# Decode attention block on one core: slots laid on multiples of 512 bytes, and the bias columns taken out of the first load

## The chip, the cores and the metric

The kernel runs on one core of one Trainium2 chip. The metric is the device time of one launch in microseconds (us). Before the change it is 1057.04 us, the median of 3 runs (1056.93 to 1057.11). About a difference of 0.2% can be told from no change.

## The reference

One token goes through a transformer block whose scales and shifts come from a condition vector `c`. All data are float32. Cut to what matters:

```python
mod = (silu(c) @ w_mod).reshape(1, 6, 1, 640)      # sa, ca, ga, sb, cb, gb
h = layernorm(x) * (1 + ca) + sa
q = (h @ wq), 32 heads of 192
p = softmax(q . k_cache * 192**-0.5)               # k_cache: 32 heads x 8192 keys x 192
x = x + ga * ((p . v_cache) @ wo)                  # v_cache: the same size
h = layernorm(x) * (1 + cb) + sb
x = x + gb * (relu(h @ w1 + b1)**2 @ w2 + b2)      # 640 -> 1536 -> 640
```

The two caches are 403 MB of the 452 MB that are read. Each byte of them is used once.

## The kernel before, in words

**Slots.** All large operands pass through three buffers, the slots (pool `strm`, 56,832 bytes in each of 128 partitions). They are filled in turn, by one DMA each or by a few: `first_t` (weights of the first modulation, the first pair's query weights, and small columns), then `k0`, `v0`, `k1`, `v1` and so on through 32 heads, then the weights of the second half. A slot is loaded again when what lay in it has been used. The pools are laid out in the order in which they are opened: `const` first, so the slots begin at byte 36,640 of a partition, which is 71 x 512 + 288.

**Issue order.** SP (SyncE) issues every DMA, in the order of the code: lines 63 (`first_t`), 95 (keys) and 99 (values). An issue that must wait holds up all that stand behind it on SP. It waits for two sorts of things. One is the engines that still read the slot. The other is the DMA's own completion semaphore: the framework gives the DMAs of SP eight semaphores in turn (`DMAHW0` to `DMAHW7` in the order of instructions below). The ninth DMA takes the first one's semaphore again, and is issued only when that first DMA has landed.

**Start.** When `first_t` has landed, ScalarE, VectorE and TensorE make the modulation, the layernorm and the first query `qb` (lines 163 to 197). VectorE then copies out `x` and the biases `bbc` over 32 lanes and transposes them (`spread`, lines 107 to 113, called on 198 and 199); they are first needed in the second half. Then comes the first head.

**A head.** VectorE multiplies the keys by the query in place (line 214), GpSimd folds part of the products (215), VectorE and ScalarE sum them (218 to 222); softmax (225 to 241); TensorE multiplies by the values (243 to 260); `own` and `turn` gather the head's output. The key slot is free after the sums on line 222, and the value slot after TensorE's last product on line 258.

**The biases** `B_b1` and `B_b2` (17 columns) are the last columns of `first`, and line 169 copies them into `bbc`.

Of the kernel before, what the change touches and what calls it, by code (L numbers as in the profile page):

```python
# [8 lines left out]
F32 = mybir.dt.float32  # L9
# [4 lines left out]
P = 128  # L14
D = 640
# [7 lines left out]
KB = DG // 32  # L23
FB = FG // 32
# [5 lines left out]
WQ = KB * PW  # L30
ROW = KV + WO
WM = KB * 2 * D
VEC = 3 * KB + FB
DA = 128
DB = DH - DA
REP = 8
# [6 lines left out]


@with_exitstack
def block_kernel(ctx: ExitStack, tc: tile.TileContext, first, kx, vx, wm1, w1, w2, out):
    nc = tc.nc
    const = ctx.enter_context(tc.tile_pool(name="const", bufs=1))
    strm = ctx.enter_context(tc.tile_pool(name="strm", bufs=3))
    work = ctx.enter_context(tc.tile_pool(name="work", bufs=2))  # L50
    psum = ctx.enter_context(tc.tile_pool(name="psum", bufs=1, space=bass.MemoryType.PSUM))
    ctx.enter_context(tc.manual_schedule())
# [1 line left out]
    def slot(name):  # L54
        return strm.tile([P, ROW], F32, tag="slot", name=name, bufs=3)

    def big(name, n):
# [4 lines left out]
    first_t = slot("first_t")  # L62
    nc.sync.dma_start(first_t[:, :WM + WQ + VEC], first)

# [1 line left out]
    make_identity(nc, ident)  # L66
    ones = const.tile([P, P], F32, name="ones")
    nc.vector.memset(ones, 1.0)
    eps_t = const.tile([P, 1], F32, name="eps_t")
    nc.vector.memset(eps_t, EPS)  # L70

    mask = const.tile([P, 2 * 512], F32, name="mask")
# [3 lines left out]
                            axis=AX.X, op=ALU.add)  # L76
# [3 lines left out]
                            axis=AX.X, op=ALU.add)  # L80
# [3 lines left out]

    vec = first_t[:, WM + WQ:WM + WQ + VEC]
    c_c = vec[:, :KB]
    x_c = const.tile([P, KB], F32, name="x_c")
    bbc = const.tile([P, FB + KB], F32, name="bbc")

    def load_k(h):  # L90
        k_t[h] = slot(f"k{h}")
        n = K_PARTS.get(h, 1)
        cuts = [KV * c // n for c in range(n)] + [ROW if h in WO_AT or h in WQ_AT else KV]
        for a, b in zip(cuts, cuts[1:]):
            nc.sync.dma_start(k_t[h][:, a:b], kx[h, :, a:b])
# [63 lines left out]
            nc.vector.scalar_tensor_tensor(to, w[:, j], s[:, j:j + 1], to, op0=ALU.mult, op1=ALU.add)  # L159

    load_k(0)

    e = const.tile([P, KB], F32, name="silu")
    nc.scalar.activation(e, c_c, AF.Exp, scale=-1.0)
# [1 line left out]
    nc.vector.reciprocal(e, e)  # L166
    nc.vector.tensor_mul(e, e, c_c)
    nc.vector.tensor_copy(x_c, vec[:, KB:2 * KB])
    nc.vector.tensor_copy(bbc, vec[:, 2 * KB:])

    ca1 = const.tile([P, KB], F32, name="ca1")
    sa = const.tile([P, KB], F32, name="sa")
# [268 lines left out]
```

## Time and profile before

| | |
|---|---|
| median of 3 runs | 1057.04 us |
| profiled execution, its own time | 1056.98 us |
| its span, first to last instruction | 1055.2 us |
| read from HBM | 451.82 MB, 428 GB/s over the span |
| DMA queue's share of 16 engines | 99.3% |
| VectorE busy | 904.1 us (86%) |
| TensorE busy, mean granted clock | 368.2 us (35%), 0.652 |

The profile is of one execution. Its own time is 1.8 us longer than its span, and 0.06 us under the median. "Share of 16 engines" adds up the times of the packets over the core's sixteen DMA engines. Where a row ends in `<-X`, the engine stood idle until X had ended. SPq is SP's queue of DMA issues, and a row of it is the issue alone, not the transfer.

### The profile page before, as it was taken

What the parts mean: (1) busy time and instruction counts of PE and PEld (TensorE: products, weight loads), DVE (VectorE), ACT (ScalarE), POOL (GpSimd) and SP (SyncE); (2) the same over time, 40 slices, a digit from 0 to 9 for tenths busy, and PEclk for the clock granted to TensorE, in tenths of its full rate; (3) what the DMA queues carried; (4) which work ended last, traced back from release to release, by engine and by line L of the source; (5) the groups of instructions that cost most, each with busy time, mean ns of one, the idle gap of its engine ahead of it and who ended that gap; (6) DMA issues with size and microseconds to landing.
All of it is one profiled execution on the core that took longest, in us unless ns stands there. A gap on an engine that the chain in (4) does not pass through costs nothing.

```text
span 1055.2 us, 5497 instructions
## 1 busy us (share of the span) xinstructions
PE 368.2 (35%) x2120; PEld 133.4 (13%) x2120; DVE 904.1 (86%) x398; ACT 89.4 (8%) x360; POOL 199.4 (19%) x44
## 2 busy tenths in 40 slices
PE   1224333243431334343143432224343133433346
PEld 0101101011110111111011110101111011110113
DVE  7887898998989989898998988989898998989982
ACT  1010000000000000000000000000000000012230
POOL 0220222220122221122221022221022222022110
PEclk9666656666665666656666665666666566666568
DMA  9999999999999999999999999999999999999997
GB/s 403 437 438 422 438 433 429 441 420 443 419 443 430 428 437 437 418 445 431 424 443 431 426 431 436 432 437 426 437 425 440 430 436 428 432 429 431 432 426 314
DMA packets 10834, 452.16 MB, mean 429 GB/s; under 512 B 1205, under 2 KB 1209, under 8 KB 1593
## 3 DMA queue, kind: packets, MB, share of 16 engines
q1 hardware_dynamic: 10808, 451.83, 99.3%
q8 instruction: 16, 0.26, 0.1%
q14 instruction: 10, 0.07, 0.0%
HBM read 451.82 MB, written 0.00 MB: 428 GB/s over the span
## 4 chain that ended last, share of the span: by engine, by line
DMA 39%; DVE 35%; PE 14%; POOL 9%; issue 1%; ACT 1%; POOLq 0%; SPq 0%; DVEq 0%; ACTq 0%
DMA k<-in_kx 36%; DVE k L214 21%; POOL k L215 9%; PE ps_o L254 9%; DVE sc L222 5%; DVE os L281 3%; PE ps_o L258 3%; DMA w_t<-in_w 2%; DVE own L277 2%; DVE sc L219 1%; DMA first_t<-in_first 1%; PE ps_mx L229 1%; PE ps_oT L287 1%; DVE ma_w L152 1%; PE ps_q L193 1%
## 5 line engine op out<-in xcount | busy, mean ns | idle before, releaser
L214 DVE TENSOR_TENSOR k<-k,qb 128x12288 f32<-128x12288 f32 (+2 forms) x37 | 415.4, 11227 | 88.6 <-DMA k<-in_kx 84.4
L215 POOL TENSOR_TENSOR k<-k 128x2880 f32<-128x2880 f32 (+2 forms) x37 | 198.1, 5354 | 813.7 <-DVE k L214 762.8
L229 PE MATMUL ps_mx<-ident,mp 128*128 128x128 f32 x32 | 15.2, 474 | 587.2 <-DVE mp L227 587.2
L219 DVE TENSOR_REDUCE sc<-k 128x32 f32<-128x6144 f32 (+5 forms) x37 | 201.5, 5445 | 1.3
L254 PE MATMUL ps_o<-v,p 128*32 128x512 f32 x1024 | 186.4, 893 | 2.6 <-ACT p L237 2.6
L222 DVE TENSOR_REDUCE sc<-k 128x30 f32<-128x2880 f32 (+2 forms) x37 | 99.7, 2696 | 5.2 <-POOL k L215 4.7
L218 ACT ACTIVATE jk<-k 128x192 f32<-128x192 f32 x127 | 44.5, 351 | 519.7 <-DVE k L214 508.5
L229 PEld LDWEIGHTS ps_mx<-ident,mp 128*128 128x128 f32 x32 | 5.8, 182 | 611.9 <-DVE mp L227 590.9
L281 DVE TENSOR_REDUCE os<-own 128x128 f32<-128x512 f32 x64 | 63.9, 1038 | 1.1
L258 PE MATMUL ps_o<-v,p 128*32 128x512 f32 x496 | 58.6, 592 | 0.0
L254 PEld LDWEIGHTS ps_o<-v,p 128*32 128x32 f32 x1024 | 40.6, 155 | 118.3 <-issue 114.9
L193 PE MATMUL ps_q<-k,ln_h 128*128 128x384 f32 x150 | 52.3, 496 | 0.2 <-DMA k<-in_kx 0.2
L237 ACT ACTIVATE p<-sc,nm 128x512 f32<-128x512 f32 x32 | 23.1, 721 | 321.6 <-DVE nm L231 180.5
L159 DVE SCALAR_TENSOR_TENSOR acc<-k,oT,acc 128x640 f32<-128x640 f32 x45 | 41.5, 923 | 1.1
L287 PE MATMUL ps_oT<-ones,os 128*128 128x1 f32 x96 | 27.2, 356 | 42.5 <-DVE os L281 30.3
L193 PEld LDWEIGHTS ps_q<-k,ln_h 128*128 128x128 f32 x150 | 27.3, 189 | 28.2 <-issue 10.9
L287 PEld LDWEIGHTS ps_oT<-ones,os 128*128 128x128 f32 x96 | 23.3, 304 | 50.3 <-DVE os L281 32.9
L231 DVE TENSOR_REDUCE nm<-ps_mx 128x1 f32<-128x128 f32 x32 | 9.3, 292 | 18.3 <-PE ps_mx L229 18.3
L218 ACT ACTIVATION_READ_ACCUMULATOR jk<-k 128x1 f32 x127 | 23.7, 187 | 0.0
L258 PEld LDWEIGHTS ps_o<-v,p 128*32 128x32 f32 x496 | 14.9, 110 | 40.0 <-issue 40.0
L277 DVE SCALAR_TENSOR_TENSOR own<-ps_o,mask 128x1024 f32<-128x1024 f32 x16 | 19.4, 1215 | 0.0
L277 DVE SCALAR_TENSOR_TENSOR own<-ps_o,ri,mask 128x1024 f32<-128x1024 f32 x15 | 19.2, 1277 | 0.0
(91 smaller groups left out, 126.5 us busy)
## 6 DMA issues: line engine op xcount, KB each, us to landing
k<-in_kx SPq DMA_DIRECT2D x28, 7104.0 KB, 27.3
v<-in_vx SPq DMA_DIRECT2D x32, 6144.0 KB, 22.7
k<-in_kx SPq DMA_DIRECT2D x2, 6144.0 KB
k<-in_kx SPq DMA_DIRECT2D x2, 4032.0 KB, 26.5
k<-in_kx SPq DMA_DIRECT2D x2, 3072.0 KB, 17.3
first_t<-in_first SPq DMA_DIRECT2D x1, 4173.5 KB, 12.7
wm_t<-in_wm SPq DMA_DIRECT2D x1, 3840.0 KB
w_t<-in_w SPq DMA_DIRECT2D x1, 3840.0 KB, 19.2
```

Of the source, the lines that this page charges most:

```text
L159: nc.vector.scalar_tensor_tensor(to, w[:, j], s[:, j:j + 1], to, op0=ALU.mult, op1=ALU.add)
L193: nc.tensor.matmul(ps[:, :PW], h1[:, b:b + 1].to_broadcast([P, P]), w[:, b], start=(b == 0), stop=(b == KB - 1))
L214: nc.vector.tensor_mul(pr, pr, q[:, None, :].to_broadcast([P, n, DH]))
L215: nc.gpsimd.tensor_add(pr[:, a:b, :DH // 2], pr[:, a:b, :DH // 2], pr[:, a:b, DH // 2:])
L218: nc.scalar.activation(jk, pr[:, i], AF.Copy, accum_out=s[:, i:i + 1])
L219: nc.vector.tensor_reduce(s[:, :a], pr[:, :a], axis=AX.X, op=ALU.add)
L222: nc.vector.tensor_reduce(s[:, a:b], pr[:, a:b, :DH // 2], axis=AX.X, op=ALU.add)
L254: nc.tensor.matmul(oa[32 * g:32 * (g + 1)], p[:, 4 * c:4 * c + 4].rearrange("p e r -> p (e r)"), t[:, 512 * c:512 * (c + 1)], start=(c < G ...
L258: nc.tensor.matmul(ob[32 * g:32 * (g + 1)], p[:, 8 * c:8 * c + 8, ::2].rearrange("p e r -> p (e r)"), t[:, 512 * (na + c):512 * (na + c + ...
L277: nc.vector.scalar_tensor_tensor(m, o, scale, mask, op0=ALU.mult, op1=ALU.mult)
L281: nc.vector.tensor_reduce(r, m[:, lo:hi].rearrange("p (j d) -> p d j", d=r.shape[1]), axis=AX.X, op=ALU.add)
L287: nc.tensor.matmul(pt[:, j:j + 1], os_[:, P * j:P * (j + 1)], ones[:, :1], start=True, stop=True)
```

## The change

1. **Layout.** A new pool `base` is opened first and holds only `eps_t`, on 384 bytes; then come the slots, and `const` after them. The slots now begin at byte 16,896 of a partition, 33 x 512; their size, 111 x 512 bytes, is as before. The tiles in `const` and `work` get other addresses.
2. **Bias columns.** They leave `first` (8,330 columns in place of 8,347) and become an input `bb` of their own. It is read by sixteen DMAs of 8, 1, 2, 3, ... 15 rows of 68 bytes, issued on SP behind `k0` and ahead of `v0`, straight into `bbc`. VectorE's copy on line 169 goes.

```diff
-VEC = 3 * KB + FB
+VEC = 2 * KB
...
+    base = ctx.enter_context(tc.tile_pool(name="base", bufs=1))
+    eps_t = base.tile([P, 96], F32, name="eps_t")[:, :1]
+    strm = ctx.enter_context(tc.tile_pool(name="strm", bufs=3))
     const = ctx.enter_context(tc.tile_pool(name="const", bufs=1))
-    strm = ctx.enter_context(tc.tile_pool(name="strm", bufs=3))
     work = ctx.enter_context(tc.tile_pool(name="work", bufs=2))
...
-    eps_t = const.tile([P, 1], F32, name="eps_t")
     nc.vector.memset(eps_t, EPS)
...
     load_k(0)
+    r0 = 0
+    for n in [8] + list(range(1, 16)):
+        nc.sync.dma_start(bbc[r0:r0 + n], bb[r0:r0 + n])
+        r0 += n
...
     nc.vector.tensor_copy(x_c, vec[:, KB:2 * KB])
-    nc.vector.tensor_copy(bbc, vec[:, 2 * KB:])
...
-        "first": np.concatenate([rows(wm[:, :2 * D], KB), wq[0], column(c, KB), column(A_x, KB),
-                                 column(B_b1, FB), column(B_b2, KB)], axis=1),
+        "first": np.concatenate([rows(wm[:, :2 * D], KB), wq[0], column(c, KB), column(A_x, KB)], axis=1),
...
+        "bb": np.concatenate([column(B_b1, FB), column(B_b2, KB)], axis=1),
```

SP's issues at the start of the program before, with the semaphores that each waits for in brackets (`DMAHW0` to `DMAHW7` are those of the DMAs; the others are the engines'):

```order
L63 DMA first_t_69<-in_first 128x8347
L95 DMA k0_88<-in_kx 128x14208
L99 DMA v0_152<-in_vx 128x12288
L95 DMA k1_205<-in_kx 128x12288 [waits DVE_49,DMAHW0_49,PE_49,Activation_49]
L99 DMA v1_207<-in_vx 128x12288 [waits DVE_49,DMAHW1_49,PE_49,Activation_49]
```

The first three have nothing to wait for. The same queue now, from the seventh small load (the ninth DMA) to `k1`; ahead of these stand `first_t`, `k0` and the small loads of 8 and of 1 to 5 rows, which wait for nothing:

```order
L165 DMA bbc_90<-in_bb 6x17 [waits DMAHW0_49]
L165 DMA bbc_90<-in_bb 7x17 [waits DMAHW1_49]
L165 DMA bbc_90<-in_bb 8x17 [waits DMAHW2_49]
L165 DMA bbc_90<-in_bb 9x17 [waits DMAHW3_49]
L165 DMA bbc_90<-in_bb 10x17 [waits DMAHW4_49]
L165 DMA bbc_90<-in_bb 11x17 [waits DMAHW5_49]
L165 DMA bbc_90<-in_bb 12x17 [waits DMAHW6_49]
L165 DMA bbc_90<-in_bb 13x17 [waits DMAHW7_49]
L165 DMA bbc_90<-in_bb 14x17 [waits DMAHW0_49]
L165 DMA bbc_90<-in_bb 15x17 [waits DMAHW1_49]
L100 DMA v0_170<-in_vx 128x12288 [waits DMAHW2_49]
L96 DMA k1_223<-in_kx 128x12288 [waits DVE_49,DMAHW3_49,PE_49,Activation_49]
```

`DMAHW0` is `first_t`'s semaphore and `DMAHW1` is `k0`'s, so the load of 6 rows waits for `first_t` and the load of 7 rows waits for `k0`; `v0`, which was third, is now nineteenth. On VectorE, the place between the spread of `x` and the first product of keys, before:

```order
L110 COPY x_t_c<-x_c 128x160
L112 STREAM_TRANSPOSE x_t<-x_t_c 128x160 [waits DVE_49]
L110 COPY bbt_c<-bbc 128x544 [waits DVE_49]
L112 STREAM_TRANSPOSE bbt<-bbt_c 128x544 [waits DVE_49]
L214 TENSOR_TENSOR k_88<-k_88,qb_142 128x12288 [waits DMAHW1_49,Activation_49]
```

and now:

```order
L111 COPY x_t_c<-x_c 128x160
L113 STREAM_TRANSPOSE x_t<-x_t_c 128x160 [waits DVE_49]
L111 COPY bbt_c<-bbc 128x544 [waits DMAHW4_49,DMAHW3_49,DMAHW5_49,DMAHW2_49,DMAHW6_49,DMAHW1_49,DMAHW7_49,DMAHW0_49,DVE_49]
L113 STREAM_TRANSPOSE bbt<-bbt_c 128x544 [waits DVE_49]
L218 TENSOR_TENSOR k_91<-k_91,qb_160 128x12288 [waits Activation_49]
```

The order is the same, but the copy of the biases, ahead of the first product, now waits for all sixteen small loads.

## Rows read from the trace of the kernel before

**Rows 1.** The page: busy time of each engine, and the DMA queue's bytes and share.
```profile
PE 368.2 (35%) x2120; PEld 133.4 (13%) x2120; DVE 904.1 (86%) x398; ACT 89.4 (8%) x360; POOL 199.4 (19%) x44
...
q1 hardware_dynamic: 10808, 451.83, 99.3%
```

**Rows 2.** Chain that ended last, in order of time: start us, us, what.
```profile
0.74 12.69 DMA first_t<-in_first
...
154.31 12.97 DVE k L214
...
217.10 12.97 DVE k L214
...
1026.98 24.16 DMA w_t<-in_w
```

**Rows 3.** DMA issues from 0 to 45 us: KB each, us to landing.
```profile
k<-in_kx SPq DMA_DIRECT2D x1, 7104.0 KB, 29.0
v<-in_vx SPq DMA_DIRECT2D x1, 6144.0 KB, 43.1
...
first_t<-in_first SPq DMA_DIRECT2D x1, 4173.5 KB, 12.7
```

**Rows 4.** SP's queue from 0 to 70 us: start us, us, what.
```profile
0.74 0.40 SPq L63 DMA_DIRECT2D first_t<-in_first  x1
1.20 0.41 SPq L95 DMA_DIRECT2D k<-in_kx  x1
1.65 0.43 SPq L99 DMA_DIRECT2D v<-in_vx  x1
31.03 0.33 SPq L95 DMA_DIRECT2D k<-in_kx  x1
54.26 0.33 SPq L99 DMA_DIRECT2D v<-in_vx  x1
64.47 0.33 SPq L95 DMA_DIRECT2D k<-in_kx  x1
```

**Rows 5.** SP's queue near the end, same columns.
```profile
1025.66 1.75 SPq L334 DMA_DIRECT2D w_t<-in_w  x4
1052.44 0.65 SPq L395 DMA_DIRECT2D out_y<-y  x1
```

**Rows 6.** First two microseconds after the first issue, busy time by stretch.
```profile
core 0: us, PE busy (x) PEld busy (x) DVE busy (x) ACT busy (x) POOL busy (x), PEclk, DMA share, GB/s
0.74:1.74 1.00, 0.00 (x0) 0.00 (x0) 0.58 (x3) 1.00 (x1) 0.93 (x3) 1.00 0.00 0
1.74:2.74 1.00, 0.00 (x0) 0.00 (x0) 1.00 (x1) 0.27 (x1) 0.14 (x1) 1.00 2.02 534
```

**Rows 7.** Waits of SP's queue from 940 us: us in total, times, longest.
```profile
SPq L437 <- DMA out_y<-y: 0.9, 1, 0.9
```

**Rows 8.** Around the first keys' product, 24 to 34 us, in order of time.
```profile
25.75 0.72 DVE L110 COPY bbt_c<-bbc 128x544 f32<-128x544 f32 x1
...
26.51 0.74 DVE L112 STREAM_TRANSPOSE bbt<-bbt_c 128x544 f32<-128x544 f32 x1
...
30.47 3.09 PEld L193 LDWEIGHTS ps_q<-k,ln_h 128*128 128x128 f32 x10
...
30.99 0.49 ACT L195 ACTIVATE qb<-ps_q 128x384 f32<-128x384 f32 x1 [11.12 <-PE ps_q L193]
...
31.52 12.96 DVE L214 TENSOR_TENSOR k<-k,qb 128x12288 f32<-128x12288 f32 x1 [4.26 <-ACT qb L195]
```

**Rows 9.** Waits of the whole span: the products for keys, SP for the slots.
```profile
DVE k L214 <- DMA k<-in_kx: 84.4, 29, 5.5
...
SPq L99 <- DVE sc L222: 601.0, 31, 22.8
SPq L95 <- PE ps_o L258: 331.1, 30, 13.2
```

**Rows 10.** The second keys' product, in order of time.
```profile
59.29 12.96 DVE L214 TENSOR_TENSOR k<-k,qb 128x12288 f32<-128x12288 f32 x1 [3.92 <-DMA k<-in_kx]
```

More of the change, by code (lines that the diff above doesn't have):

```diff
@@ L45, in block_kernel @@
 @with_exitstack
-def block_kernel(ctx: ExitStack, tc: tile.TileContext, first, kx, vx, wm1, w1, w2, out):
+def block_kernel(ctx: ExitStack, tc: tile.TileContext, first, kx, vx, wm1, w1, w2, bb, out):
     nc = tc.nc
+    base = ctx.enter_context(tc.tile_pool(name="base", bufs=1))
+    eps_t = base.tile([P, 96], F32, name="eps_t")[:, :1]
+    strm = ctx.enter_context(tc.tile_pool(name="strm", bufs=3))
     const = ctx.enter_context(tc.tile_pool(name="const", bufs=1))
-    strm = ctx.enter_context(tc.tile_pool(name="strm", bufs=3))
     work = ctx.enter_context(tc.tile_pool(name="work", bufs=2))
```

## The prediction

> **What bounds the kernel now.** I read the page first. The DMA queue's packets fill 99.3% of sixteen engines' span, VectorE is busy 86% and TensorE 35% [rows 1]. The reader is to see there that the rings, as I call the sixteen engines' queues of packets, are never empty from the first load to the last weights. The chain in order of time says the same from the other side: it begins with the landing of `first_t`, passes through the loads of keys head after head, and ends in a load of weights of 24.16 us [rows 2]. The waits explain why VectorE, though 86% busy, is not the bound: before its products for keys it waits 84.4 us for the keys, 29 times, 2.9 us each, while SP stands 601.0 and 331.1 us waiting for slots to come free [rows 9]. A slot comes free some microseconds before the transfer in progress ends, so an issue is always ready in time. What this kernel pays for is therefore bytes over the pace of the rings, and any time in which the rings are empty. Nothing later gives an empty stretch back.
>
> The pace: a pair of heads from the chain, 154.31 to 217.10 us, takes 62.79 us for 2 x (7104 + 6144) KB, 432.1 GB/s [rows 2, 3]. The first keys landed at 1.20 + 29.0 = 30.20 us, `first_t` at 13.44 and `v0` at 1.65 + 43.1 = 44.75 [rows 3, 4]: 13,248 KB in 31.31 us, 433.3 GB/s.
>
> **The sixteen loads and SP.** Three issues stand at the start before, 0.455 us apart (0.74, 1.20, 1.65), and then SP waits until 31.03 [rows 4]. After the change eight DMAs go out freely, by about 6 us; all the small ones among them stand behind `k0` on the rings. The ninth waits for `first_t`'s semaphore, 13.44 us: no harm, the rings hold `k0`. The tenth, of 7 rows, waits for `k0`'s semaphore, which has its last count at 30.20; TensorE's first weight load from `k0` at 30.47 agrees [rows 8]. Until then SP can issue nothing more, and `v0` stands nine issues behind. But at 30.20 the rings hold only the last small rows. So they run dry, which they do nowhere before the end of the trace of before.
>
> How long? First the issues. A DMA of 128 rows costs SP 0.455 us from start to start. The only DMA of few rows, the output of 4, took 0.65 us where issues that also begin with a wait took 0.33 [rows 4, 5]: 0.32 more. The four pieces of `w2`, of 128 rows but as small as 320 KB, took 0.44 each (1.75 over 4) [rows 5], so few bytes are not the reason and few rows may be. [...] I take 0.455 + 0.32 = 0.775 us each, with 0.455 as the other end. Nine small loads (7 to 15 rows) at 0.775 are 7.0 us: `v0` is issued at 30.2 + 7.0 = 37.2. Their own semaphore waits do not bind: a small load lands some 1.7 us after its issue (output: issued at 1052.44, 0.65 for the issue, 0.9 of waiting until it landed, and the steps between [rows 5, 7]), and the load of 15 rows, which waits for that of 7, has its turn 6 us later.
>
> Then the start on empty rings. From the first issue the engines moved nothing for 1.0 us and all were busy in the next [rows 6]. `first_t` needed 12.7 us from issue to landing, of which 4173.5 KB at 433.3 GB/s are 9.86: 2.84 us beside the transfer. The output needed 1.7 with next to no transfer. These are the bounds of a restart. `v0`, 14.5 us of transfer, lands at 37.2 + 14.5 + 1.7 to 2.84 = 53.4 to 54.5 in place of 44.75: 8.65 to 9.8 us late. I take the middle, 9.2. With issues at 0.455 it is 9 x 0.32 = 2.9 less, 6.3.
>
> The loads' own traffic is 128 rows of 68 bytes, taken out of `first_t`'s rows: nothing as bytes. As packets they lie in the dry stretch, which covers several microseconds of them; the output's four rows of 640 bytes were through within the 0.9 us that SP waited for them [rows 7], so without that cover sixteen such, one behind the other on one engine, would cost it between next to nothing and 16 x 0.9 = 14 us. I take nothing.
>
> **VectorE.** The copy of the biases, 0.72 us, and the transpose, 0.74, ran at 25.75 to 27.25, in the idle time before the first product at 31.52, which waited for `qb` [rows 8]. Now the copy waits for the last load: issued at 30.2 + 8 x 0.775 = 36.4, landed at 38.1; copy and transpose end at 39.6. Behind it on VectorE stand the first product of keys and the whole first head, for which GpSimd, ScalarE, TensorE's softmax and SP's next slots wait: 8.1 us late. This costs no more than the rings already lost. `v1`'s issue moves from 54.26 to 62.4 and must come before `k1` ends: `k1` landed by 59.29 [rows 10], now by 68.5, 6 us later than the issue. `k2`'s issue moves from 64.47 [rows 4] to 72.6, some 10 us before `v1` ends. From there each head waits for its keys as before, and all runs 9.2 us later. The line 169 copy that goes (under 0.2 us, ahead of the first query) is nothing: the first product no longer waits for `qb`.
>
> **The slots' address.** No row shows a transfer into an aligned slot. All slots lay at 288 past a multiple of 512, all the time. What the rows bound is how much faster such a transfer was ever seen: 433.3 against 432.1 GB/s, 0.28% of 1040 us, 2.9 us; that is the one end. The other is nothing; a loss from the other addresses of `const` would be VectorE's, which has 2.9 us a head to spare. I take 0.5, near the end of nothing, since 432.1 and 433.3 were reached at the same address.
> [...]
>
> **Sum.** 1056.98 (own time of the profiled execution, 1055.2 of span and 1.8 around it) + 9.2 - 0.5 = 1065.7. The runs' median lies 0.06 above that execution, which changes nothing.
>
> **Rivals.**
> 1. The same dry stretch, but issues of few rows cost 0.455 us as the others do, and the 0.65 was the output's own. For it: one row is thin. Against it: no other issue among the rows is over 0.45. 1056.98 + 6.3 - 0.5 = 1062.8.
> 2. Not slower: SP is not held. The tenth DMA's wait ends well before 30 us. Then all issues are out by 0.74 + 18 x 0.775 = 14.7 us, the rings never run dry, and only VectorE starts late: the small rows land just behind `k0`, at about 30.5, copy and transpose end at 32.0, 0.5 us behind the old start of 31.52, hidden by the 4 us that `v1`'s issue stood ahead of `k1`'s end (54.26 and a start of 1.0, against 59.29). The time is 1056.98 - 0.5 = 1056.5. It decides if SP issues `v0` before about 29 us. Against it: the order shows the wait on `DMAHW1`, and the same kind of wait on SP held every slot's reuse before.
> 3. Not slower: the aligned slots speed every transfer. To cancel 9.2 us the pace must rise from 432.1 by 0.9% to 436 GB/s, past the best stretch seen; at 433.3 the time is 1065.7 - 2.4 = 1063.3, still slower. At 436 it is 1057.
> 4. Slower still: a row of 68 bytes costs an engine as much as the output's whole way, 1.7 us. The engine that has a row of each of the sixteen loads then takes 16 x 1.7 = 27 us, of which the dry stretch and the time behind `k0` cover about 9: 1065.7 + 18 = 1084. Against it: the eight rows that each engine has of `first_t` came through in 12.7 us in all [rows 3], at the full pace but for 2.84 us, so the way is paid once for rows that follow each other, not for each row. It is the least likely.
>
> **Chances.** Forecast 0.72, rival 1 0.12, rival 2 0.06, rival 3 0.06, rival 4 0.04. A measurement of this kernel tells about 0.2%, 2.1 us, from no change. Forecast and rivals 1 and 4 are slower: 0.88. Rivals 2 and 3 are mostly within 0.2%: 0.08 the same and 0.04 faster. The range of the forecast is 1063.5 to 1067.5 by its own bounds (8.65 to 9.8 for the restart, 0 to 2.9 for the pace); to hold 8 in 10 it reaches down to rival 1: 1061.0 to 1068.0.
>
> **What would show it.** In the profile after: SP's queue has a gap up to about 30.2 us, then nine issues of `bbc` at 0.7 to 0.8 us each, and `v0` at about 37; the DMA row of the stretch 31 to 38 us reads near nothing; the first product of keys starts at about 39.6 behind the spread of the biases; everything later reads like before, 9 us later, at 432 GB/s or slightly more. If `v0` is issued before 30 us the forecast is wrong in its main term; if it comes at 34, rival 1 holds; if the pace between two heads rises to 436, the layout was mis-sized.

## The result, and the profile after

The changed kernel takes **1059.86 us**, the median of 7 runs (1059.74 to 1060.24), against 1057.05 us before (7 runs): a ratio of 1.0027, with a 95% interval of 1.0017 to 1.0038. It is slower, by 2.8 us, where 8.7 us were forecast. The profiled execution of after took 1060.24 us, 0.4 above its median and 3.3 us more than that of before.

The page of after, which answers to [rows 1] (busy time and share of each engine; the DMA queue's packets, MB and share):

```profile
span 1058.5 us, 5516 instructions
...
PE 369.6 (35%) x2120; PEld 134.4 (13%) x2120; DVE 904.0 (85%) x397; ACT 89.4 (8%) x360; POOL 199.4 (19%) x44
...
q1 hardware_dynamic: 11064, 451.83, 98.9%
...
HBM read 451.82 MB, written 0.00 MB: 427 GB/s over the span
```

The same bytes; the rings are busy 98.9% of a longer span instead of 99.3%. VectorE has the same 904 us of work. So the page points to the rings, and does not say where.

SP's issues of the first 70 us, against [rows 4] (start us, duration us, what):

```profile
0.74 0.39 SPq L65 DMA_DIRECT2D first_t<-in_first  x1
1.19 0.42 SPq L96 DMA_DIRECT2D k<-in_kx  x1
1.65 31.74 SPq L165 DMA_DIRECT2D bbc<-in_bb  x16
33.44 0.39 SPq L100 DMA_DIRECT2D v<-in_vx  x1
34.01 0.35 SPq L96 DMA_DIRECT2D k<-in_kx  x1
58.73 0.33 SPq L100 DMA_DIRECT2D v<-in_vx  x1
```

`v0`, issued at 1.65 us before, is issued at 33.44. The row of sixteen hides the two waits; the same queue in three pieces, 1.6 to 13 us, 13.2 to 30.05 and 30.05 to 33.4 (all of the last nine):

```profile
1.65 2.00 SPq L165 DMA_DIRECT2D bbc<-in_bb  x6
13.38 0.27 SPq L165 DMA_DIRECT2D bbc<-in_bb  x1
30.09 3.30 SPq L165 DMA_DIRECT2D bbc<-in_bb  x9
```

Six go out at once, one at 13.38 when `first_t` has landed, and the rest from 30.09, when `k0` has landed. That is the hold that was forecast. But the nine held issues take 3.30 us, 3.35 with the step to `v0` (30.09 to 33.44): 0.37 each, not 0.775.

SP's waits (total us, times, longest) name what it stood for at that line:

```profile
SPq L100 <- DVE sc L226: 600.8, 31, 24.2
...
SPq L165 <- DMA k<-in_kx: 16.4, 1, 16.4
...
SPq L165 <- DMA first_t<-in_first: 9.7, 1, 9.7
```

What the rings did (length of the stretch, busy time of each engine, granted clock, DMA share, GB/s). A row of a transfer counts whole in the stretch in which it starts, so a share can be over 1, and a stretch near 0 is one in which no row begins:

```profile
core 0: us, PE busy (x) PEld busy (x) DVE busy (x) ACT busy (x) POOL busy (x), PEclk, DMA share, GB/s
29.00:30.00 1.00, 1.00 (x3) 0.60 (x2) 0.00 (x0) 0.00 (x0) 0.00 (x0) 1.00 0.05 2
30.00:34.20 4.20, 4.20 (x13) 2.16 (x12) 0.00 (x0) 0.49 (x1) 0.00 (x0) 1.00 0.03 2
34.20:36.00 1.80, 0.20 (x1) 0.00 (x0) 1.36 (x2) 0.00 (x0) 0.00 (x0) 1.00 1.36 437
```

From 30.0 to 34.2 us the rings moved 2 GB/s, the small rows alone. In the trace of before they were full there:

```profile
29.00:36.00 7.00, 5.18 (x15) 2.64 (x13) 4.48 (x1) 0.49 (x1) 0.00 (x0) 1.00 1.04 449
```

By the packet records of after, the last rows of `k0` end on the sixteen engines between 29.00 and 29.79 us (mean 29.30), and the first rows of `v0` start between 34.44 and 35.66 (mean 34.71). So an engine is without a large row for 5.4 us on average; before, `v0`'s rows follow within 0.002 us (means 29.324 and 29.326).

VectorE at the start of the first head, against [rows 8, 10]:

```profile
34.60 0.72 DVE L111 COPY bbt_c<-bbc 128x544 f32<-128x544 f32 x1 [8.96 <-DMA bbc<-in_bb]
35.36 0.74 DVE L113 STREAM_TRANSPOSE bbt<-bbt_c 128x544 f32<-128x544 f32 x1
36.03 12.92 DVE L218 TENSOR_TENSOR k<-k,qb 128x12288 f32<-128x12288 f32 x1
...
65.43 12.96 DVE L218 TENSOR_TENSOR k<-k,qb 128x12288 f32<-128x12288 f32 x1 [5.59 <-DMA k<-in_kx]
```

The copy of the biases waited 8.96 us for the small loads and the first product starts at 36.03 instead of 31.52. The second head's product waits for `k1` as it did before, and starts at 65.43 instead of 59.29: **6.14 us late**. This start marks when `v0` and `k1` have both landed, so it measures what the rings have lost by then.

Twenty-seven heads later, the product of keys of head 28, of after and then of before:

```profile
912.26 12.96 DVE L218 TENSOR_TENSOR k<-k,qb 128x12288 f32<-128x12288 f32 x1 [1.62 <-DMA k<-in_kx]
```

```profile
908.36 12.96 DVE L214 TENSOR_TENSOR k<-k,qb 128x12288 f32<-128x12288 f32 x1 [1.67 <-DMA k<-in_kx]
```

Now it is 3.90 us late, and at the end 3.3 us. Between head 1 and the end nearly 3 us have come back, a little in every head. The chain (start us, us, what) shows it against [rows 2]:

```profile
1.19 28.88 DMA k<-in_kx
...
33.01 1.42 DMA bbc<-in_bb
...
160.66 12.97 DVE k L218
...
223.18 12.97 DVE k L218
```

This pair of heads takes 62.52 us here (160.66 to 223.18), 62.79 before; from head 1 to head 28 the gain is 0.17 us a pair on average. The first two lines are new: the landing of `k0`, for which SP was held, and that of the last small load are now on the chain.

What comes back can be read from the records of the DMA packets, one for each row of a transfer (128 for `k0`). Counted here are the rows of 49,152 bytes that start after 65 us of the span (some 4,050 in each kernel; the mean is of those under 1850 ns, which leaves out 28 in each kernel):

```
kernel                      slots at     median ns   over 1821 ns   mean ns
before                      288 mod 512    1819          28%         1820.5
after                       0              1815           1%         1815.1
```

The rows of 56,832 bytes are 4.6 ns shorter in after and the smaller ones 2 to 5; over the some 560 rows that an engine carries after 65 us this sums to 2.8 us. Up to 64 us the rows of 49,152 bytes of before had a median of 1815 ns too.

### The profile page after: what moved, and what is told of

It reads as the page before. It is cut to its first block, busy times and chain, and to the rows that moved or that the text cites. A ratio compares the mean times of both kernels' runs of the same rounds, so it can differ in the third digit from the quotient of the medians.

```text
span 1058.5 us, 5516 instructions
## 1 busy us (share of the span) xinstructions
PE 369.6 (35%) x2120; PEld 134.4 (13%) x2120; DVE 904.0 (85%) x397; ACT 89.4 (8%) x360; POOL 199.4 (19%) x44
## 3 DMA queue, kind: packets, MB, share of 16 engines
q1 hardware_dynamic: 11064, 451.83, 98.9%
## 4 chain that ended last, share of the span: by engine, by line
DMA 40%; DVE 34%; PE 14%; POOL 9%; issue 1%; ACT 0%; SPq 0%; POOLq 0%; DVEq 0%; ACTq 0%
DMA k<-in_kx 38%; DVE k L218 21%; PE ps_o L258 9%; POOL k L219 9%; DVE sc L226 5%; DVE os L285 3%; PE ps_o L262 3%; DMA w_t<-in_w 2%; DVE own L281 2%; DVE sc L223 1%; PE ps_mx L233 1%; PE ps_oT L291 1%; DVE nm L235 0%; PE ps_y L394 0%; DVE os L275 0%
```

## The experiments

All times are medians, taken on a chip beside the kernel before, which stayed at 1057.01 to 1057.05 us. "Behind" counts from there, and a ratio is to that kernel, with its 95% interval in brackets.

**Each part alone.** The first kernel has the new pools alone:

```diff
+    base = ctx.enter_context(tc.tile_pool(name="base", bufs=1))
+    eps_t = base.tile([P, 96], F32, name="eps_t")[:, :1]
     strm = ...
     const = ...
```

> The first part of the change alone: pool base first, slots on multiples of 512 bytes; the biases stay columns of the first load. Theory A (the address speeds every transfer into a slot): in the trace after, the rows of 49,152 bytes have a median of 1815 ns where before had 1819 with a quarter at 1826, some 5 ns over 555 rows of each engine or 3 us, so the time falls to 1054. Theory B (the rows are faster because the sixteen loads or the restart on empty rings shifted the engines against each other): without the loads the time stays at 1057.

Measured: **1053.71 us**, ratio 0.9969 (0.9958 to 0.9981). The products of keys of heads 1 and 28 in its trace:

```profile
59.52 12.96 DVE L215 TENSOR_TENSOR k<-k,qb 128x12288 f32<-128x12288 f32 x1 [4.29 <-DMA k<-in_kx]
...
906.36 12.96 DVE L215 TENSOR_TENSOR k<-k,qb 128x12288 f32<-128x12288 f32 x1 [1.64 <-DMA k<-in_kx]
```

At head 1 it is 0.2 us behind the kernel before, at head 28 2.0 us ahead, at the end 3.0 in the profiled runs. The rows of 49,152 bytes have a median of 1815 ns, 1% over 1821. Theory A holds.

The second has the sixteen loads alone (the pools of before, the loads and the input `bb` of after).

> The second part alone: sixteen loads behind the first keys, slots at 288 past a multiple of 512 as before. Both theories see v0 issued at about 33.4 us and the rings dry for 5 us and slow to start. Theory A: nothing is given back, 1057 + 5.7 = 1062.7. Theory B: the rows run at 1815 ns here too, 1060.

Measured: **1063.46 us**, ratio 1.0062 (1.0048 to 1.0076); rows with a median of 1819 ns, 27% over 1821. Heads 1 and 28:

```profile
65.32 12.96 DVE L217 TENSOR_TENSOR k<-k,qb 128x12288 f32<-128x12288 f32 x1 [5.54 <-DMA k<-in_kx]
...
914.61 12.96 DVE L217 TENSOR_TENSOR k<-k,qb 128x12288 f32<-128x12288 f32 x1 [1.67 <-DMA k<-in_kx]
```

6.03 us behind at head 1, 6.25 at head 28: nothing is given back, and the time is 0.8 us above theory A's 1062.7. Theory B, that the loads or the restart made the rows faster, falls. The two parts add up within the intervals: -3.3 + 6.4 = +3.1, against +2.8 for both.

**Is it the hold?** The whole change, but with six small loads:

```diff
-    for n in [8] + list(range(1, 16)):
+    for n in (24, 24, 20, 20, 20, 20):
```

> The whole change with the 128 rows of biases in six loads (24, 24, 20, 20, 20, 20 rows) in place of sixteen, at the same place: v0 is the ninth DMA and waits for the semaphore of the first load alone. Theory of the held issue: v0 is issued by about 14 us, the rings never run dry, the 5.7 us go; with theory A the time is 1054, with theory B 1057 (no restart, and loads that are nearly even). Rival: the small rows themselves, on the rings behind k0, cost the time; then it stays at 1060.

Measured: **1053.82 us**, ratio 0.9970 (0.9958 to 0.9981). SP's first issues, and the products of heads 0 and 1:

```profile
1.65 2.60 SPq L165 DMA_DIRECT2D bbc<-in_bb  x6
13.46 0.36 SPq L100 DMA_DIRECT2D v<-in_vx  x1
```

```profile
32.53 12.92 DVE L218 TENSOR_TENSOR k<-k,qb 128x12288 f32<-128x12288 f32 x1
59.21 12.96 DVE L218 TENSOR_TENSOR k<-k,qb 128x12288 f32<-128x12288 f32 x1 [2.88 <-DMA k<-in_kx]
```

`v0` goes out at 13.46 us, when the first semaphore is free. The 128 small rows are still on the rings behind `k0`, and the first product still starts 1.0 us later than before (32.53), yet head 1 starts on time at 59.21. So neither the small rows nor VectorE's start 1.0 us late costs anything that shows; the loss is the late issue of `v0`. The rival falls.

**How much of it is the wait, how much the issues?** With seven small loads `v0` is itself the tenth DMA:

```diff
-    for n in [8] + list(range(1, 16)):
+    for n in (20, 20, 20, 20, 16, 16, 16):
```

> The whole change with seven small loads (four of 20 rows, three of 16) in place of sixteen: v0 is now the tenth DMA and is itself the one that waits for k0's semaphore, with no small load held ahead of it. Theory (the loss is a restart plus nine held issues of 0.37 us, 3.35 us in the trace after): v0 is issued at 30.1 instead of 33.4, the rings are dry for about 1 us and start slowly, and the time is 1053.8 (the six loads) + 6.1 - 3.35 = 1056.5. Rival (the rings lose nothing by a wait for k0's semaphore alone, all the loss is the row of small loads): 1053.8. Rival (the wait alone is the loss, the nine issues are not): 1060.

Measured: **1056.98 us**, ratio 0.9998 (0.9989 to 1.0007), 3.2 us behind the six loads. SP's issues, the rings in three stretches of 1 us, and the product of head 1:

```profile
1.65 12.27 SPq L165 DMA_DIRECT2D bbc<-in_bb  x7
30.34 0.35 SPq L100 DMA_DIRECT2D v<-in_vx  x1
```

```profile
29.00:30.00 1.00, 1.00 (x3) 0.39 (x3) 0.00 (x0) 0.00 (x0) 0.00 (x0) 1.00 0.15 9
30.00:31.00 1.00, 1.00 (x3) 0.62 (x2) 0.00 (x0) 0.00 (x0) 0.00 (x0) 1.00 0.00 0
31.00:32.00 1.00, 1.00 (x4) 0.57 (x3) 0.90 (x2) 0.39 (x1) 0.00 (x0) 1.00 2.37 737
```

```profile
62.05 12.96 DVE L218 TENSOR_TENSOR k<-k,qb 128x12288 f32<-128x12288 f32 x1 [5.76 <-DMA k<-in_kx]
```

No small issue is held ahead of `v0`, which goes out at 30.34. The stretches say only that no large row starts between 29 and 31 us; the packet records say how long the engines lack one. The last rows of `k0` end between 29.07 and 29.99 us (mean 29.30), and the first of `v0` start between 31.32 and 32.08 (mean 31.49): 2.2 us on average, 1.04 until `v0` is issued and 1.15 from there. Then the first row of `v0` on each engine takes 2.53 us instead of 1.82, 0.7 more. Together that is 2.9 us, and head 1 starts at 62.05, 2.84 us behind the six loads. So a stop and restart of the rings alone costs about 2.8 us; both rivals fall.

After is 3.38 us later still at head 1 (65.43), and its nine held issues took 3.35. The same count in after gives 5.41 us without a large row and 0.64 for the slow first rows (2.46 us each instead of 1.82), 6.05 for the 6.14 by which head 1 is late, so under 0.1 is left for the small rows and for VectorE's late start. By the medians of the runs the split is 3.2 for the restart and 2.9 for the issues, and the seven loads took 0.5 us more than the 1056.5 expected.

**Do the uneven numbers of rows matter?**

```diff
-    for n in [8] + list(range(1, 16)):
+    for n in [8] * 16:
```

> The whole change with sixteen loads of 8 rows each in place of 8 and 1 to 15. The same eight semaphores hold v0 behind nine small loads. In the trace after, an issue of 8 rows stood 0.34 us before the next and the nine 0.37 on average: v0 is issued 0.3 us earlier, 1059.6. Rival (the uneven numbers of rows do something of their own to the engines, for good or ill): off that by 1 us or more.

Measured: **1059.67 us**, ratio 1.0026 (1.0016 to 1.0036), 0.2 us less than after, whose runs it overlaps. `v0` is issued at 33.05, 0.4 us earlier. The numbers of rows have no effect of their own that these runs can tell.

**Address, or merely another order of pools?** The first experiment also moved `const` and `work`. Here they are moved and the slots lie where they did within 512 bytes:

```diff
-    eps_t = base.tile([P, 96], F32, name="eps_t")[:, :1]
+    eps_t = base.tile([P, 168], F32, name="eps_t")[:, :1]
```

> As the first experiment, but the tile in pool base is 288 bytes longer, so that the slots lie at 288 past a multiple of 512 as before, while const and work stand behind the slots as after. Theory A: 1057, no gain. Rival (the new addresses of const and work bring the gain, through the engines): 1054.

Measured: **1057.02 us**, ratio 1.0000 (0.9992 to 1.0009). So the gain does not come from the order of the pools. `const` and `work` too lie 288 bytes further than in the first experiment, so the time alone does not single out the slots; but VectorE is busy for 904.2 us here and 904.1 there, and the rows written into the slots are slow again (the line for 288 in the table below).

**Which multiple?** The same line with 160, 112, 104 and 128 columns:

> The layout alone, slots at 256 past a multiple of 512, biases in the first load. If only a multiple of 512 counts: 1057. If a multiple of 256 or of 64 is enough: 1053.7.

> The layout alone, slots at 64 past a multiple of 512. If a multiple of 64 is enough: 1053.7. If 256 or 512 is needed: 1057, rows with a median of 1819 ns.

> The layout alone, slots at 32 past a multiple of 512 (before: 288, which is also 32 past a multiple of 64 and of 256). If what counts is the place within 64 or within 256 bytes: 1057 as before. If 288 was bad by itself and a small offset costs in proportion: between 1053.7 and 1057.

> The layout alone, slots at 128 past a multiple of 512. If a multiple of 256 is needed: about 1056.5 to 1057, rows with a median of 1818 or 1819 ns. If a multiple of 128 is enough: 1053.8.

Measured, with the rows of 49,152 bytes counted as above:

```
slots at (mod 512)   us        ratio to before (95%)        median ns   over 1821   mean ns
0                    1053.71   0.9969 (0.9958 to 0.9981)      1815          1%       1815.1
256                  1053.81   0.9968 (0.9956 to 0.9981)      1815          1%       1815.1
128                  1056.30   0.9993 (0.9984 to 1.0002)      1819         22%       1818.8
64                   1056.52   0.9995 (0.9986 to 1.0004)      1818         28%       1819.4
32                   1056.98   0.9999 (0.9991 to 1.0008)      1819         28%       1820.5
288                  1057.02   1.0000 (0.9992 to 1.0009)      1819         28%       1820.4
```

Slots at 256 give the whole gain, as those at 0 do. The medians at 128 and 64 lie 0.5 to 0.7 us under the kernel before, each of their 11 runs is below every run of it beside them, and their rows' means go the same way; their intervals still reach 1. 288 was not bad by itself: 32 does the same.

The layout alone (1053.71), or the layout with six loads (1053.82), beats both kernels.

## Why the prediction was wrong

The direction was right, and so was the mechanism of the loss: `v0` behind the semaphore of `k0`, the rings dry, nothing of the stop recovered by another engine. The size was not: +8.7 forecast, +2.8 measured, outside the stated range. (The forecast's own bounds, 8.65 to 9.8 less 0 to 2.9, give 1062.7 to 1066.8, not the 1063.5 to 1067.5 that it states; the measured time lies outside both.) Three terms of the sum:

- **Issues of few rows: 7.0 us forecast, 3.35 measured.** This is the largest miss. The step failed where the output's 0.65 us, a single row of the trace, was taken as the price of few rows; that was an estimate, and the runs show no such price. In the trace after, a small issue is no dearer than one of 128 rows (nine held ones take 3.30 us, 0.37 each; those of `k` and `v` take 0.33 to 0.42 each). The other end that was kept, 0.455, was too high as well. Among the nine, the step to the next issue grows from 0.31 us at 7 rows to 0.43 at 15. Why the output's issue takes 0.65 us, which differs also in writing to HBM, was not tried.
- **The restart: 2.2 us forecast, 2.8 measured.** The forecast was the middle between `first_t` (2.84 us beside its transfer) and the output (1.7). Seven loads measured it alone, 2.84 us at head 1. The packets show what it is made of: `k0`'s last rows end 1.04 us before `v0` can be issued, its own first rows start 1.15 us after that, and these rows take 0.7 us longer. The nearest row of before was the one with the same kind of transfer, `first_t`; the middle was a poor choice.
- **The slots' address: 0.5 us of gain forecast, 3.3 measured.** The two ends were 0 and 2.9, and the value was put near the end of nothing because both paces, 433.3 and 432.1 GB/s, had been seen at the same address. That was no reason: the first was seen at the start alone, and the aligned slots keep it for the whole run. After 65 us the rows of 49,152 bytes take 1815.1 ns on average in after and 1820.5 in before (the means counted above), which over sixteen engines is 433.3 and 432.0 GB/s.

With the measured terms: 3.35 + 2.8 - 3.3 = +2.85.

**Of the rivals**, rival 1 had the mechanism with a cheaper issue, 1062.8, and was still too high, since it kept 0.5 us for the address. Rival 3, the address, was the other half of the answer: it was priced as if it had to cancel the loss alone (436 GB/s) and got a chance of 0.06. The forecast took the rivals as alternatives; here a cheap form of 1 and a strong form of 3 held together. Rivals 2 and 4 fell: SP was held, and the small rows cost nothing (six loads; in after a row of 68 bytes took an engine 0.011 us on average).

**Right, point by point.** SP's gap ended at 30.09 us (30.2 forecast); the semaphore waits of the held loads among themselves did not bind; the first product came behind the biases, late by 4.5 us (8.1 forecast, with the dearer issues) and without a cost, for VectorE then stood idle for 5.59 us until `k1` came; the copy of line 169 that went shows nowhere.

**Open.** Why a row into a slot at 32, 64, 128 or 288 is slower than one at 0 or 256 was not found, nor why it is so only after a time: before, the rows ran at 1815 ns up to about 64 us, but with the sixteen loads alone up to about 86 us, and at 64 and 128 past a multiple of 512 most of them up to about 78. So 65 us is no fixed time, and no experiment was made for it.

## What to carry to other kernels

Where a kernel is bound by its DMA rings, count the DMAs between a large load and the next against the number of semaphores that the queue uses in turn, eight here: small loads squeezed in between can hold the next large one until an earlier one has landed (`v0` was issued at 33.44 us instead of 1.65), and the restart of the empty rings comes on top (2.8 us). Try the buffers of large loads on multiples of 256 bytes, by ordering the pools; here slots at 0 and 256 past a multiple of 512 gave 0.3%, for a few hundred bytes of a partition. And when two parts of a change have opposite signs, sum their ends, rather than pricing each as a rival that must win alone.

## What was not expected of the hardware

- The issue of a small DMA on SP mostly took less time the fewer rows it had. From start to start, out of the trace after: 0.27 us for 1 row, 0.31 for 7, 0.34 for 8, 0.43 for 15 (0.46 for 128 rows). The first load of 8 and that of 3 rows stand out with 0.42 and 0.40.
- A stop of the rings cost 2.8 us though no small load was held: with seven loads the engines lacked a large row for 2.2 us on average, and the first rows afterwards took 2.53 us instead of 1.82.
- A row of 49,152 bytes written into a slot at 288 or at 32 past a multiple of 512 took 5.4 ns more on average than one at 0, 0.3%: the median is 4 ns more, and 28% of the rows are over 1821 ns. At 64 and 128 the mean was 4.3 and 3.7 ns more, at 256 the same as at 0.
